# A last sum spread 16 partitions apart: one copy and a store of eight runs in place of four copies and a store of two rows

## The chip, the core and the metric

The kernel runs on one core of a Trainium2 chip. The metric is the device time of one execution in microseconds (us); the median over several runs counts, and a smaller one is better. The core's engines each work through their own queue in order: TensorE (PE; PEld for its weight loads), VectorE (DVE), ScalarE (ACT), GpSimd (POOL) and SyncE (SP), which here issues transfers. Data lies in DRAM, in SBUF (128 partitions) and in PSUM (128 partitions, where PE writes its sums).

## The reference

Two batch rows `x` of 448 numbers are normalised to `xn`. Then

- A: one decode step of attention with 16 query heads, 8 key and value heads of 256, over the last 4096 positions of the caches: `q = xn @ wq`, `softmax(q k / 16) v`, then `@ wo` (4096 x 448).
- B: a dense layer with the mish activation: `h = xn @ w1 + b1` (1792 wide), `h * tanh(softplus(h))`, then `@ w2` (1792 x 448).

The output is `x + A + B`, two rows of 448 in bf16. The K and V windows, the weights and little else are read: 77.67 MB.

## The kernel before, in words

All loads of K, V and the weights are issued by SP, in the order in which the code stands (the kernel runs under a manual schedule: each engine takes its instructions in program order). Three ring buffers of 32 KB a partition hold K, V, wq, w1 and w2 in turn.

The attention runs over four units `u` (0 to 3), each with two of the eight heads for both batch rows. For a unit, `turns` transposes K on VectorE (L275), `scores` multiplies (L362), takes the exponential on ScalarE and transposes the result, `weigh` sums the denominators, `values` multiplies with V (L408), `gather` brings the parts together, and `finish` (L450) divides and writes the bf16 tile `oT` on VectorE (L453). For the first three units `relay` and `mix_early` put the product with wo into the PSUM tile `early` (2 x 448), which also starts with `x`.

The end of the kernel uses a second PSUM tile, `acc` (L238). The 448 output columns are cut into G = 4 groups of 112, and group g stands in partitions 32g and 32g + 1, one for each batch row, so that the four groups' matmuls use four column groups of PE. `carry` (L240) copies `early` into `acc` through a 2 x 2 identity `id2`. `add_rows` (L253) adds a product: for each group a matmul whose fixed operand `lhsT` has 128 partitions and 2 columns and whose moving operand is 112 columns of a weight. It is called by `mix` (L495) for the last unit (8 calls, 32 matmuls) and by `dense_out` (L566) for w2 (14 calls, 56 matmuls). `dense_in` and `mish` have made `act_bf` (L502, L550) long before. w2 comes in four parts (L553, L561): 7, 4, 2 and 1 blocks of 448 columns, the last being the last load of all.

Behind the last matmul, `acc` is copied into the tile `res` (2 x 448, bf16) in four pieces of 2 x 112, two by VectorE (L626) and two by ScalarE (L628), and SP stores `res` (L629).

Of the kernel before, what the change touches and what calls it, by code (L numbers as in the profile page):

```python
# [9 lines left out]
ALU = mybir.AluOpType  # L10
AXIS = mybir.AxisListType
BF16 = mybir.dt.bfloat16
FP32 = mybir.dt.float32
# [4 lines left out]
def kernel(  # L18
# [13 lines left out]
    nc = tc.nc  # L32
    P = 128
    G = 4
# [4 lines left out]
    Bsz, Sq, D = A_x.shape  # L39
# [3 lines left out]
    rep = Hq // Hkv  # L43
# [3 lines left out]
    KU = J // Bsz  # L47
    U = Hkv // KU
# [12 lines left out]
    F2 = F // 2  # L61
    NI = F2 // P
    DG = D // G
    assert Sq == 1 and Bsz == 2 and rep == 2 and Dh == 256 and G * DG == D and Hq == 16
    assert W == 4096 and D == 448 and F == 1792
    scale = float(Dh) ** -0.5
# [9 lines left out]
    consts = ctx.enter_context(tc.tile_pool(name="consts", bufs=1))  # L76
    small = ctx.enter_context(tc.tile_pool(name="small", bufs=2))
# [32 lines left out]
    def load_wo(u):  # L110
# [22 lines left out]
        out=wq[:, 0 : NS * HW], in_=A_wq.flatten().rearrange("(p e) -> p e", p=P)  # L133
# [4 lines left out]
    ident = consts.tile([P, P], BF16)  # L138
# [6 lines left out]
    nc.vector.tensor_copy(  # L145
        out=halves[:], in_=ident[0:2, 0:2].unsqueeze(2).to_broadcast([2, 2, Bsz])
    )
    id2 = consts.tile([Bsz, Bsz], FP32)
    nc.vector.tensor_copy(out=id2[:], in_=ident[0:Bsz, 0:Bsz])
    hot = consts.tile([P, KU, 4, rep, 32, KU], BF16)  # L150
    nc.gpsimd.memset(hot[:], 0.0)
    for k in range(KU):
        nc.gpsimd.tensor_copy(
            out=hot[:, k, :, :, :, k],
            in_=ident[:].rearrange("p (q y) -> p y q", y=4).unsqueeze(2)
# [11 lines left out]
        out=rstd[:], in_=mv[:, 1:2], func=ACT.Sqrt, bias=eps_t[:], scale=1.0  # L167
# [4 lines left out]
        out=xn_bf[:],  # L172
        in0=x_bf[:],
# [7 lines left out]
        out=parm[:], in_=ident[:].rearrange("p (a o) -> p o a", o=2), axis=AXIS.X, op=ALU.add  # L181
# [3 lines left out]
        out=jm[:],  # L185
        in_=ident[:].rearrange("p (a j h) -> p j a h", j=J, h=rep),
        axis=AXIS.XY,
        op=ALU.add,
    )
    nc.vector.tensor_scalar(  # L190
        out=jm[:], in0=jm[:], scalar1=-1.0, scalar2=29952.0, op0=ALU.add, op1=ALU.mult
# [3 lines left out]
        out=mneg[:], in_=jm[:].unsqueeze(1).to_broadcast([P, TH * 8, J])  # L195
    )
    sel = consts.tile([P, 2, NQ], FP32)
    for x in range(2):
        for w in range(4):
            at = 32 * w + (2 * (w % 2) + x) * NQ  # L200
            src = ident[:, at : at + NQ]
            if w == 0:
                nc.vector.tensor_copy(out=sel[:, x, :], in_=src)
            else:
                nc.vector.tensor_tensor(
                    out=sel[:, x, :], in0=sel[:, x, :], in1=src, op=ALU.add
# [16 lines left out]
    for odd in range(2):  # L223
        for half in range(2):
            o = (half + odd) % 2
            nc.vector.tensor_scalar(
                out=xs[:, odd::2, half * Bsz : (half + 1) * Bsz],
                in0=xr_ps[:, odd::2, :],
# [8 lines left out]
    )  # L237
    acc = ps_a.tile([P, DG], FP32)  # L238

    def carry():  # L240
        e_sb = small.tile([P, 2 * Dh], FP32, tag="vs", name="e_sb", bufs=1)[0:Bsz, 0:D]
        nc.scalar.copy(out=e_sb, in_=early[:])
        for g in range(G):
            nc.tensor.matmul(
                acc[32 * g : 32 * g + Bsz, :],
                lhsT=id2[:],
                rhs=e_sb[:, g * DG : (g + 1) * DG],
                start=True,
                stop=False,
                skip_group_check=True,  # L250
            )

    def add_rows(lhsT, rows, stop=False):  # L253
        for g in range(G):
            nc.tensor.matmul(  # L255
                acc[32 * g : 32 * g + Bsz, :],
                lhsT=lhsT,
                rhs=rows[:, g * DG : (g + 1) * DG],
                start=False,
                stop=stop,  # L260
                skip_group_check=True,
            )
# [20 lines left out]
    for n in range(2):  # L283
        for e in range(2):
# [3 lines left out]
                out=sp[:],  # L288
                in_=ident[:, o : o + 63 : 2].unsqueeze(1).to_broadcast([P, G, 32]),
# [91 lines left out]
    state = {}  # L381
# [67 lines left out]

    def finish(u):  # L450
        po, rec = state.pop(("o", u)), state.pop(("rec", u))
        oT = small.tile([P, 2, KU * rep, Bsz], BF16, tag="oT", name="oT")
        nc.vector.tensor_tensor(  # L453
            out=oT[:].rearrange("p c k b -> p c b k"),
            in0=po[:].rearrange("p c (b k) -> p c b k", b=Bsz),
            in1=rec[:].rearrange("p (b k) -> p b k", b=Bsz).unsqueeze(1)
            .to_broadcast([P, 2, Bsz, KU * rep]),
            op=ALU.mult,
        )
        state["oT", u] = oT  # L460
# [34 lines left out]
    def mix(u):  # L495
        oT, w = state.pop(("oT", u)), wo_t.pop(u)
        for k2 in range(KU):
            for h in range(rep):
                for c in range(2):
                    add_rows(oT[:, c, k2 * rep + h, :], w[:, k2, h, c * D : (c + 1) * D])  # L500

    act_bf = consts.tile([P, NI, 2, Bsz], BF16)  # L502

    def load_w1():
        t = ring("w1")
# [29 lines left out]
    def mish():  # L535
        h_ps = state.pop("h")
        shape = [P, NI, 2, Bsz]
        u_sb = consts.tile(shape, FP32, name="u_sb")
        nc.scalar.activation(out=u_sb[:], in_=h_ps[:], func=ACT.Exp)
        t_sb = consts.tile(shape, FP32, name="t_sb")  # L540
        nc.vector.scalar_tensor_tensor(  # L541
            out=t_sb[:], in0=u_sb[:], scalar=2.0, in1=u_sb[:], op0=ALU.add, op1=ALU.mult
        )
        den = consts.tile(shape, FP32, name="den_sb")
        nc.vector.tensor_scalar(
            out=den[:], in0=t_sb[:], scalar1=2.0, scalar2=None, op0=ALU.add
        )
        nc.vector.reciprocal(out=den[:], in_=den[:])
        nc.vector.tensor_tensor(out=t_sb[:], in0=t_sb[:], in1=den[:], op=ALU.mult)
        nc.vector.tensor_tensor(out=act_bf[:], in0=h_ps[:], in1=t_sb[:], op=ALU.mult)  # L550

    KH = 4096
    w2_parts = ((0, 0, NI), (1, 0, 4), (1, 4, 6), (1, 6, NI))  # L553
# [12 lines left out]
    def dense_out(part):  # L566
        k, lo, hi = w2_parts[part]
        for i in range(lo, hi):
            at = k * KH + i * D
            add_rows(  # L570
                act_bf[:, i, k, :], state["w2"][:, at : at + D], stop=(k == 1 and i == NI - 1)
            )

    load_w1()
# [3 lines left out]
    turns(0, 1)  # L578
    dense_in()
    mish()  # L580
    scores(0, 1)
    weigh(0)
    for u in range(U - 1):
        load_k(u + 1, 0)
        load_v(u, 0)
        load_k(u + 1, 1)
        load_v(u, 1)
        load_wo(u)
        turns(u + 1, 0)
        values(u, 0)  # L590
        scores(u + 1, 0)
        turns(u + 1, 1)
        values(u, 1)
        gather(u)
        finish(u)
        scores(u + 1, 1)
        relay(u)
        mix_early(u)
        if u < U - 2:
            weigh(u + 1)  # L600
    u = U - 1
# [5 lines left out]
    for part in range(len(w2_parts)):  # L607
        load_w2(part)
    carry()
    values(u, 0)  # L610
    values(u, 1, 32)
    weigh(u)
    gather(u, last=False)
    values_fixed(u, 1, 32, 56)
    values_fixed(u, 1, 56, TV)
    finish(u)
    mix(u)
    for part in range(len(w2_parts)):
        dense_out(part)

    res = consts.tile([Bsz, D], BF16)
    for g in range(G):
        dst = res[:, g * DG : (g + 1) * DG]
        src = acc[32 * g : 32 * g + Bsz, :]
        if g % 2 == 0:
            nc.vector.tensor_copy(out=dst, in_=src)  # L626
        else:
            nc.scalar.copy(out=dst, in_=src)  # L628
    nc.sync.dma_start(out=out.flatten_outer_dims(), in_=res[:])  # L629


# [28 lines left out]
```

## Time and profile before

| | us |
|---|---|
| median of 4 runs | 189.36 |
| lowest and highest | 189.24, 189.54 |
| the profiled execution | 189.48 |
| its span | 187.5 |
| busy: VectorE, PE, ScalarE, GpSimd | 92.9, 74.3, 12.4, 4.7 |
| moved | 77.78 MB, 415 GB/s |

The span is the stretch from the first to the last instruction that the profiler recorded in one execution; the device time contains 1.98 us around it. A row of 40 digits shows busy tenths in 40 equal slices of the span, some 4.7 us each. A group's row gives line, engine, operation, output tile, input, count and nanoseconds; views of one line or tile give the shortest, median and longest of its instructions. A name with a small q (SPq) is the queue of an engine, which issues transfers or waits. Matmuls are pipelined, and their ends are modelled. The chain of waits is followed back from the last instruction: at each step to what released it.

### The profile page before, as it was taken

The page shows a single profiled execution, that of the slowest core. Times are in us where ns is not written, and L with a number is a line of the kernel's source. Part 1 is how long each engine was busy: PE and PEld are TensorE (multiplying, and loading weights), DVE is VectorE, ACT ScalarE, POOL GpSimd, SP SyncE. Part 2 cuts the span into 40 slices and gives each one's busy share as a digit, 9 for nine tenths or more (in the row PEclk, how much of TensorE's full clock was granted, in tenths as well). Part 3 has the DMA queues.
Part 4 walks back from the last instruction along what each step waited for, and adds up shares of the span by engine and source line. Part 5 has one row for each costly group of instructions (what it writes and reads, how often), then busy time and mean ns, then how long its engine had stood idle before and what let it go on. Part 6 is the DMA issues. An engine that isn't in the chain of part 4 may idle for free.

```text
span 187.5 us, 1952 instructions
## 1 busy us (share of the span) xinstructions
PE 74.3 (40%) x852; PEld 34.4 (18%) x856; DVE 92.9 (50%) x93; ACT 12.4 (7%) x26; POOL 4.7 (2%) x16
## 2 busy tenths in 40 slices
PE   0300367593119000882047002870068005854763
PEld 0100122451003000340012001430022002422452
DVE  6719624974792098028940395048910592040101
ACT  3000030101000100110001000110001000120101
POOL 8100000000000000000000000000000000000000
PEclk9999999999999955699559855798556655899555
DMA  6999999999999999999999999999999999999991
GB/s 225 447 420 398 469 399 426 469 444 447 413 420 413 430 449 389 471 447 447 440 406 409 420 447 415 452 444 447 447 427 406 413 433 427 440 423 398 432 404 43
DMA packets 4451, 77.78 MB, mean 415 GB/s; under 512 B 470, under 2 KB 1244, under 8 KB 2012
## 3 DMA queue, kind: packets, MB, share of 16 engines
q1 hardware_dynamic: 4436, 77.66, 96.8%
q8 instruction: 6, 0.10, 0.2%
q14 instruction: 1, 0.01, 0.0%
q10 hardware_dynamic: 8, 0.01, 0.0%
HBM read 77.67 MB, written 0.00 MB: 414 GB/s over the span
## 4 chain that ended last, share of the span: by engine, by line
DMA 79%; DVE 12%; PE 4%; issue 3%; SPq 1%; DVEq 0%
DMA k<-in_A_k_cache_dram 44%; DMA v<-in_A_v_cache_dram 23%; DMA w<-in_B_w_dram 12%; DVE kt L275 12%; PE pv L408 4%; PE acc L255 1%; SPq L98 0%; SPq L132 0%; SPq L561 0%; DVEq L655 0%; DVE res L626 0%; DVE t_sb L541 0%
## 5 line engine op out<-in xcount | busy, mean ns | idle before, releaser
L275 DVE STREAM_TRANSPOSE kt<-k 128x4096 f32<-128x4096 f32 x16 | 70.1, 4417 | 35.6 <-DMA k<-in_A_k_cache_dram 35.5
L408 PE MATMUL pv<-v,p 128*32 128x512 bf16 x240 | 24.1, 571 | 73.5 <-DMA v<-in_A_v_cache_dram 73.5
L408 PEld LDWEIGHTS <-p 128*32 128x32 bf16 x240 | 8.7, 129 | 86.6 <-issue 63.4
L362 PE MATMUL sc<-kt,qd 128*32 128x512 bf16 x256 | 20.1, 457 | 1.8 <-DVE qd L330 1.4
L453 DVE TENSOR_TENSOR oT<-o,rec 128x16 bf16<-128x16 f32 x4 | 0.7, 175 | 23.5 <-PE o L426 19.1
L373 DVE STREAM_TRANSPOSE p<-ex 128x512 bf16<-128x512 bf16 x8 | 5.2, 690 | 10.8 <-ACT ex L370 10.8
L370 ACT ACTIVATE ex<-sc 128x512 bf16<-128x512 f32 x8 | 4.8, 597 | 75.6 <-PE sc L362 75.6
L362 PEld LDWEIGHTS <-qd 128*32 128x32 bf16 x256 | 6.9, 107 | 12.3 <-issue 6.9
L297 PE MATMUL q_ps<-wq,xs 128*32 128x512 bf16 x28 | 3.2, 629 | 13.2 <-DMA wq<-in_A_wq_dram 13.2
L394 DVE TENSOR_REDUCE rec<-dn 128x8 f32<-128x512 f32 x4 | 2.8, 692 | 11.2 <-PE dn L386 9.8
L420 ACT COPY vs<-pv 128x512 f32<-128x512 f32 x4 | 2.3, 585 | 56.9 <-PE pv L408 56.9
L426 PE MATMUL o<-sel,vs 128*128 128x8 f32 x32 | 5.2, 289 | 2.1 <-ACT vs L420 2.1
L426 PEld LDWEIGHTS o<-sel,vs 128*128 128x128 f32 x32 | 4.8, 228 | 5.5 <-ACT vs L420 5.5
L487 PE MATMUL early<-wo,ox 128*2 128x448 bf16 x24 | 5.0, 352 | 1.9 <-ACT ox L478 1.9
L525 PE MATMUL h_ps<-xs,w 128*128 128x4 bf16 x49 | 3.7, 196 | 2.3 <-DMA w<-in_B_w_dram 2.3
L386 PE MATMUL dn<-p,ones 128*128 128x512 bf16 x5 | 2.4, 526 | 4.1 <-DVE p L344 3.8
L218 PE MATMUL xr_ps<-ident,xrows 2*128 2x2 bf16 x7 | 1.0, 181 | 7.1 <-DVE xrows L217 7.1
L297 PEld LDWEIGHTS <-xs 128*32 128x32 bf16 x28 | 1.1, 137 | 14.9 <-issue 14.9
L525 PEld LDWEIGHTS <-w 128*128 128x128 bf16 x49 | 3.2, 149 | 2.5 <-DMA w<-in_B_w_dram 2.4
L351 PE MATMUL sc<-mneg,ident 128*128 128x512 bf16 x7 | 3.1, 443 | 0.0
L441 PE MATMUL o<-p,v 128*128 128x8 bf16 x64 | 1.9, 168 | 1.8 <-DMA v<-in_A_v_cache_dram 1.8
L145 DVE COPY halves<-ident 2x4 bf16<-2x4 bf16 x1 | 1.9, 1912 | 1.3 <-POOL ident masks.py:199 1.3
(67 smaller groups left out, 44.3 us busy)
## 6 DMA issues: line engine op xcount, KB each, us to landing
k<-in_A_k_cache_dram SPq DMA_DIRECT2D x8, 4096.0 KB, 27.5
v<-in_A_v_cache_dram SPq DMA_DIRECT2D x7, 4096.0 KB, 21.2
wq<-in_A_wq_dram SPq DMA_DIRECT2D x1, 3584.0 KB, 20.2
wo<-in_A_wo_dram SPq DMA_DIRECT2D x3, 896.0 KB, 21.6
v<-in_A_v_cache_dram SPq DMA_DIRECT2D x1, 2048.0 KB, 17.6
w<-in_B_w_dram SPq DMA_DIRECT2D x1, 1568.0 KB, 13.0
v<-in_A_v_cache_dram SPq DMA_DIRECT2D x1, 1536.0 KB, 21.7
wo<-in_A_wo_dram SPq DMA_DIRECT2D x2, 448.0 KB
```

The source lines that it names most:

```text
L275: nc.vector.transpose(out=kt[i][:, :, r, :, :], in_=t[:, r * KE : (r + 1) * KE].bitcast(FP32).rearrange("p (a c j) -> p a c j", c=P // (R ...
L297: nc.tensor.matmul(q_ps[32 * u : 32 * (u + 1), :], lhsT=xs[:, s, :], rhs=wq_t[s][:, u * 512 : (u + 1) * 512], start=(s == 0), stop=(s == N ...
L351: nc.tensor.matmul(sc[:].rearrange("p t c m -> p (t c m)"), lhsT=ident[:], rhs=mneg[:].rearrange("p a j -> p (a j)"), start=True, stop=Fal ...
L362: nc.tensor.matmul(sc[32 * w : 32 * (w + 1)].rearrange("p t c m -> p t (c m)"), lhsT=qd[:, u, 2 * n + e, :, :].rearrange("p g q -> p (g q) ...
L370: nc.scalar.activation(out=ex[:, :, :, i, :], in_=sc[:], func=ACT.Exp, scale=scale)
L373: nc.vector.transpose(out=p_all[:, :, h * TH : (h + 1) * TH, :].rearrange("p g t q -> p t g q"), in_=ex[:, h * TH : (h + 1) * TH].rearrang ...
L386: nc.tensor.matmul(dn[:].rearrange("p a q -> p (a q)"), lhsT=ones[:], rhs=p_run[:, i].rearrange("p t q -> p (t q)"), start=(i == 0), stop= ...
L394: nc.vector.tensor_reduce(out=rec[:], in_=dn[:].rearrange("p a q -> p q a"), axis=AXIS.X, op=ALU.add)
L408: nc.tensor.matmul(pv[32 * w : 32 * (w + 1), :, :].rearrange("p x d -> p (x d)"), lhsT=p_run[:, g, 4 * a : 4 * a + 4, :].rearrange("p t q ...
L426: nc.tensor.matmul(po[:, c, :], lhsT=sb[:, x, c::2], rhs=sel[:, x, :], start=(x == 0 and c == 0), stop=(last and x == 1), skip_group_check ...
L487: nc.tensor.matmul(early[:], lhsT=ox[:, i, :], rhs=w[:, i, :], start=False, stop=(u == U - 2 and i == 7),)
L525: nc.tensor.matmul(h_ps[:, i, :, :].rearrange("p k b -> p (k b)"), lhsT=w1_v[:, s, i, :], rhs=xs[:, s, 0 : 2 * Bsz], start=False, stop=(s ...
```

## The change

The batch rows of a group now stand SP = 32 / 2 = 16 partitions apart, in partitions 32g and 32g + 16. To that end the fixed operands become tiles `[128, 2, 16]` in which the columns of batch row 0 stand in places 0 to 15 and those of row 1 in places 16 to 31, and column i is taken with the 17 columns from i to i + 16: its first is row 0's, its last row 1's, and what the 15 between add to other partitions of `acc` is not read. `id2` gets the same form with 32 columns. Unused places are set to zero by three memsets on VectorE at the start. Then partitions 0 to 112 of `acc` are copied at once, and every 16th partition of the copy is stored: eight runs of 112 numbers.

```diff
+    SP = 32 // Bsz
...
-    id2 = consts.tile([Bsz, Bsz], FP32)
-    nc.vector.tensor_copy(out=id2[:], in_=ident[0:Bsz, 0:Bsz])
+    id2 = consts.tile([Bsz, Bsz, SP], FP32)
+    nc.vector.memset(id2[:], 0.0)
+    nc.vector.tensor_copy(out=id2[:, :, 0], in_=ident[0:Bsz, 0:Bsz])
+    act_bf = consts.tile([P, Bsz, SP], BF16)
+    nc.vector.memset(act_bf[:], 0.0)
+    o_bf = consts.tile([P, Bsz, SP], BF16)
+    nc.vector.memset(o_bf[:], 0.0)
...
+    def spaced(t, i):
+        return t[:].rearrange("p b i -> p (b i)")[:, i : i + SP + 1]
...
-                acc[32 * g : 32 * g + Bsz, :],
-                lhsT=id2[:],
+                acc[32 * g : 32 * (g + 1), :],
+                lhsT=id2[:].rearrange("p b i -> p (b i)"),
...
-                acc[32 * g : 32 * g + Bsz, :],
+                acc[32 * g : 32 * g + SP + 1, :],
...
-        oT = small.tile([P, 2, KU * rep, Bsz], BF16, tag="oT", name="oT")
+        if u < U - 1:
+            oT = small.tile([P, 2, KU * rep, Bsz], BF16, tag="oT", name="oT")
+            oT_out = oT[:].rearrange("p c k b -> p c b k")
+        else:
+            oT = o_bf
+            oT_out = oT[:, :, 0 : 2 * KU * rep].rearrange("p b (c k) -> p c b k", c=2)
...
-                    add_rows(oT[:, c, k2 * rep + h, :], w[:, k2, h, c * D : (c + 1) * D])
-
-    act_bf = consts.tile([P, NI, 2, Bsz], BF16)
+                    i = (c * KU + k2) * rep + h
+                    add_rows(spaced(oT, i), w[:, k2, h, c * D : (c + 1) * D])
...
-        nc.vector.tensor_tensor(out=act_bf[:], in0=h_ps[:], in1=t_sb[:], op=ALU.mult)
+        nc.vector.tensor_tensor(
+            out=act_bf[:, :, 0 : 2 * NI].rearrange("p b (k i) -> p i k b", k=2),
+            in0=h_ps[:],
+            in1=t_sb[:],
+            op=ALU.mult,
+        )
...
-                act_bf[:, i, k, :], state["w2"][:, at : at + D], stop=(k == 1 and i == NI - 1)
+                spaced(act_bf, k * NI + i),
+                state["w2"][:, at : at + D],
+                stop=(k == 1 and i == NI - 1),
...
-    res = consts.tile([Bsz, D], BF16)
-    for g in range(G):
-        dst = res[:, g * DG : (g + 1) * DG]
-        src = acc[32 * g : 32 * g + Bsz, :]
-        if g % 2 == 0:
-            nc.vector.tensor_copy(out=dst, in_=src)
-        else:
-            nc.scalar.copy(out=dst, in_=src)
-    nc.sync.dma_start(out=out.flatten_outer_dims(), in_=res[:])
+    rows = 32 * (G - 1) + SP + 1
+    res = consts.tile([P, DG], BF16)
+    nc.vector.tensor_copy(out=res[0:rows, :], in_=acc[0:rows, :])
+    nc.sync.dma_start(
+        out=out.rearrange("b s (g d) -> g (s b) d", g=G), in_=res[0:rows:SP, :]
+    )
```

The number of matmuls, their moving operands, the loads and their order stay as they are.

More of the change, by code (lines that the diff above doesn't have):

```diff
@@ L451, in finish @@
         po, rec = state.pop(("o", u)), state.pop(("rec", u))
-        oT = small.tile([P, 2, KU * rep, Bsz], BF16, tag="oT", name="oT")
+        if u < U - 1:
[4 more added lines that the diff above has]
+            oT_out = oT[:, :, 0 : 2 * KU * rep].rearrange("p b (c k) -> p c b k", c=2)
         nc.vector.tensor_tensor(
-            out=oT[:].rearrange("p c k b -> p c b k"),
+            out=oT_out,
             in0=po[:].rearrange("p c (b k) -> p c b k", b=Bsz),
```

## The prediction

> **What bounds the kernel now.** I read the page first, for the whole span, then the chain of waits of the last 7.5 us, then the timeline of the last 3 us.
>
> ```profile
> DMA  6999999999999999999999999999999999999991
> ...
> DMA 79%; DVE 12%; PE 4%; issue 3%; SPq 1%; DVEq 0%
> ```
>
> The DMA row of the 40 slices is full from the second slice to the 39th: the transfer engines stream without a break from about 5 us to 183 us. So an edit that only lengthens or shortens an engine's work under that stream changes nothing; only what lies behind the last landing counts. The chain of waits shows that end (start, length, what):
>
> ```profile
> 160.93 22.76 DMA w<-in_B_w_dram
> 183.68 0.04 issue
> 183.72 0.54 PE acc L255 x16
> 184.27 0.03 issue
> 184.29 0.57 PE acc L255 x12
> ```
>
> The parts of w2 land at 183.68 and later, and PE starts 0.04 us behind each. The timeline from 184.5 us on shows that even these matmuls wait for landings:
>
> ```profile
> 184.29 0.53 PE L255 MATMUL acc<-w,act_bf 128*2 128x112 bf16 x12
> 184.56 0.09 PEld L255 LDWEIGHTS <-act_bf 128*2 128x2 bf16 x3
> 184.85 0.56 DVE L626 CAST res<-acc 2x112 bf16<-2x112 f32 x2 [3.27 <-PE acc L255]
> 184.89 0.51 ACT L628 CAST res<-acc 2x112 bf16<-2x112 f32 x2 [9.16 <-PE acc L255]
> 185.48 0.33 SPq L629 DMA_DIRECT2D out_dram<-res  x1
> ```
>
> The weight loads break off and start again at 184.56, where the last part (one group of four matmuls) has landed. From there the end is a plain row: four matmuls to 184.83, copies to 185.41, the store's issue from 185.48 to 185.81. In windows of 0.04 us the transfer engines then carry 22 GB/s in 186.20 to 186.28 and nothing later, and the span ends at 187.5, after the store's receipt and the shutdown. The profiled execution took 189.48 us, 1.98 us more than its span of 187.5; the median of the four runs is 189.36, 0.12 lower. I work out the difference against the profiled one and put it on the median.
>
> **The copies (removed from the end).** The view of the tile res:
>
> ```profile
> L626 DVE CAST res<-acc x2: 260/264/269, 184.9 to 185.1; 2x112 bf16<-2x112 f32 x2
> L628 ACT CAST res<-acc x2: 243/244/246, 184.9 to 185.2; 2x112 bf16<-2x112 f32 x2
> ```
>
> Two copies one behind the other on each engine take 0.56 us on VectorE and 0.51 on ScalarE, and the store waits for the later one. After the change one copy of 113x112 stands there. Does it cost more for 113 partitions? Copies out of PSUM give the answer: 128x16 takes 165 ns (L314), 2x112 takes 264, 32x256 takes 420 (L330). 96 more columns cost 99 ns and 144 more cost 156, 1.03 to 1.08 ns a column, whatever the partitions. So the new copy costs about 165 + 96 x 1.08 = 269 ns: it ends at 185.12 instead of 185.41. **Gain 0.56 - 0.27 = 0.29 us**, all of it on the path. ScalarE's copies end earlier and go too, with the store's wait for ScalarE; nothing else was behind them.
>
> The Trainium skill, page "TensorEngine Tiling (Array Packing)", section "PSUM Bottleneck", advises the opposite, to evacuate PSUM with ScalarE and VectorE both. If four copies' work stayed four copies' work on one engine, it would take 4 x 0.264 = 1.06 us, and this term would be a loss of 0.50 instead of a gain of 0.29; the rows above decide against that here.
>
> **The store (dearer).** Before, it is two rows of 896 bytes, plain on both sides. After, it is 8 runs of 224 bytes: SBUF partitions 16 apart, and on the DRAM side a nested pattern of 4 column groups x 2 rows. Its issue lies on the path. The length of an issue on SP, from the views of the lines:
>
> ```profile
> L629 SPq DMA_DIRECT2D out_dram<-res x1: 334/334/334, 185.5 to 185.5; - x1
> ...
> L98 SPq DMA_DIRECT2D k<-in_A_k_cache_dram x8: 534/535/632, 0.7 to 119.5; - x8
> ...
> L113 SPq DMA_DIRECT2D wo<-in_A_wo_dram x3: 597/597/598, 58.0 to 137.4; - x3
> ```
>
> Plain patterns (the store's two rows of 896 bytes, or w1's 128 rows of 12.5 KB, 337 ns at L506) cost 0.33 to 0.34; so neither rows nor bytes matter. Nested ones (k's 32 positions x 4 heads, wo's 64 x 2, the last wo's 128 x 2 with 462 to 586 ns at L119) cost 0.46 to 0.60. The new store is nested; I take 0.535, the median of k's 8 issues and of v's 10: **loss 0.20 us**. Ends: 0.243 (the plain bias load on ScalarE's queue, L128), a gain of 0.09; and 0.632 (the first k load), a loss of 0.30. That plain wq takes 0.575 near the start shows that the pattern is not all that decides, so a loss of nothing remains possible.
>
> Then the landing. The two old rows go by one transfer engine each, some 0.03 us apart: in the two windows 186.20 to 186.24 and 186.24 to 186.28 the share is 0.06 and 0.07, one engine of 16. Eight runs over up to eight engines put the last up to 6 x 0.03 = 0.18 us later; over four engines 2 x 0.03 = 0.06. I take **0.07 us** and keep 0 and 0.5 as ends. The 0.5 is SP's wait for the store in the view of waits, taken a second time in full, if small writes had to be answered one after the other.
>
> The skill's page "DMA: Bandwidth & Descriptors", section "Specifications", says that transfers under 512 bytes make the transfer engine read, modify and write; 896-byte rows become 224-byte runs here, so this rule speaks against the change. It gives no price, and no row here shows such a write; by it the landing would lean to its upper end and the sum to a loss.
>
> **The matmuls (17 columns instead of 2).** All 88 matmuls of L255 load 17 columns instead of 2, and four more with 32 columns stand in the carry. What the columns cost:
>
> ```profile
> L255 PEld LDWEIGHTS <-act_bf x56: 79/126/128, 182.2 to 184.6; 128*2 128x2 bf16 x56
> ...
> L408 PEld LDWEIGHTS <-p x240: 92/146/151, 47.7 to 174.1; 128*32 128x32 bf16 x120
> ```
>
> 32 columns instead of 2 cost 13 ns at the shortest and 20 at the median, so 15 more columns cost about 10. The moving side is the same 112 columns. Up to the last landing PE has pauses: it finishes 32 matmuls of L255 by 182.55 and the next 28 by 183.42, and waits for w2 until 182.60 and 183.72. A group of four takes about 0.09 us (28 matmuls, seven groups, in 0.82 us with the 0.25 of the last). Even four weight loads 10 ns longer each, with nothing of them hidden, add 0.04 a group, 0.16 us to the four groups at 183.72. Their last start is then about 184.13, before the landing at 184.29. So only the last group pays: **0.01 us** if its four column groups load side by side, with ends of 0 and 4 x 23 = 0.09 (151 less 128). Without the cover of the waits, 22 groups at 0.04 would be 0.88 us; this is the price if the landings were not the bound.
>
> **What is hidden.** At the start VectorE gets three memsets, and the copy of id2 then waits for one of them. A small memset there takes 59 ns (L159), while the neighbouring small copies take 1.9 us beside GpSimd's memsets. At worst this is 3 x 1.9 = 5.7 us in front of the layer norm and of the first K transposes. VectorE is idle for 4.35 us before those (13.21), so they could start 1.4 late; the w1 load behind them would be issued at 23.4 instead of 22.0, while the second k load keeps the queue fed until 31.33. PE needs xs at 21.8, and VectorE is done with it at 8.9. Cost 0. The strided output of act_bf (28 elements, 188 ns) is followed by 3.15 us of idle time before the next transposes: cost 0. The last oT goes to a fixed tile: the same operation of 175 ns, at 181.4 before a landing at 182.6, cost 0. The carry's four matmuls with 32 columns stand at 167.6, and the next work starts at 168.9: cost 0.
>
> **Sum.** -0.29 + 0.20 + 0.07 + 0.01 = -0.01 us: 189.47 for the profiled execution, **189.35** for the median. The copies' gain is paid back at the store.
>
> **Rivals.** A measurement of this kernel tells a difference of about 0.2% (0.38 us) from none.
> - *The store is not dearer*: the issue stays at 0.33, the landing at its place. Then the copies' gain stays: 189.36 - 0.29 = 189.07, still within 0.2%. For it speaks that L629 and L506 cost the same with 2 and 128 rows; against it, that no nested pattern in the trace is below 0.46.
> - *The store is the new bound and the kernel slower*: issue +0.26 (as wo) and small writes answered in turn, up to +0.5. With the matmuls' 0.01 that is 0.77 - 0.29 = +0.48: 189.84. It is slower by over 0.2% from a store that costs 0.67 more. For it: eight small runs instead of two; against it: two runs over different engines overlap in the windows.
> - *Faster by over 0.2%*: needs the store below its present cost, issue 0.243 and nothing else: 189.36 - 0.29 - 0.09 = 188.98. Only a plain load speaks for it.
> - *The copy does not do what is said*: if 113 partitions did cost per partition group, 1.06 us, the time would be 189.36 + 0.50 + 0.28 = 190.14; the 128x16 row speaks against it.
>
> **Numbers.** The wash (within 0.15 of 189.35) 0.56; the gain kept (189.0 to 189.2) 0.25; slower by over 0.2% through the store 0.09, through the copy 0.02; faster by over 0.2% 0.05; the last 0.03 lies between the wash and slower. So faster 0.05, same 0.84, slower 0.11. The range goes from the best store, 188.98, to 189.75, which leaves out most of the slower cases.
>
> **What would show it.** Right: one copy on VectorE of 0.25 to 0.29 us, with the store's issue starting near 185.19 if the last landing stays; that issue 0.46 to 0.60 long; the end of the span 2.2 to 2.4 us after the copy (2.05 before). Wrong: an issue of 0.33 (first rival), more than 0.3 us added between the store's packets and the end (second rival), a copy over 0.35 us, or the group of 16 at 183.72 reaching past the next landing. If the last landing itself moves by more than 0.3 us, the stream was changed by something that I have not seen here.

## The result and the profile after

| | before | after |
|---|---|---|
| median, us | 189.39 (55 runs) | 189.66 (37 runs) |
| lowest and highest | 189.18, 189.80 | 189.42, 189.91 |
| profiled execution | 189.48 | 189.77 |
| its span | 187.5 | 187.8 |

The ratio is 1.0014 with a 95% interval of 1.0009 to 1.0018: the changed kernel is slower by 0.27 us. The prediction had a change of -0.01. The loss is below the 0.2% that it called no change, and 189.66 lies inside its range (188.98 to 189.75), but the loss is clear of the measurement.

The stream is as full as before but for one of the 40 slices (8 tenths instead of 9): 77.78 MB at 414 GB/s, where it was 415.

```profile
DMA  6999999999999999999999999999999989999990
```

The end is still a plain row of steps. The timeline of the changed kernel from 184.5 us on (start, length, engine, line, operation; in brackets the idle time ahead and what ended it):

```profile
184.43 0.54 PE L264 MATMUL acc<-w,act_bf 128*17 128x112 bf16 x12
184.43 0.36 PEld L264 LDWEIGHTS <-act_bf 128*17 128x17 bf16 x11 [0.19 <-issue]
185.01 0.28 DVE L643 CAST res<-acc 113x112 bf16<-113x112 f32 x1 [3.30 <-PE acc L264]
185.31 0.68 SPq L644 DMA_DIRECT2D out_dram<-res  x1
```

One copy of 0.28 us stands where 0.56 stood, but the store's issue takes 0.68 us instead of 0.33. Where the store goes on from there is seen in the transfer engines' work, in windows (after the clock: share of the 16 engines, GB/s), of the changed kernel:

```profile
185.90:186.50 0.60, 0.00 (x0) 0.00 (x0) 0.00 (x0) 0.00 (x0) 0.00 (x0) 0.50 0.00 0
186.50:186.60 0.10, 0.00 (x0) 0.00 (x0) 0.00 (x0) 0.00 (x0) 0.00 (x0) 0.50 0.03 4
186.60:186.70 0.10, 0.00 (x0) 0.00 (x0) 0.00 (x0) 0.00 (x0) 0.00 (x0) 0.50 0.09 14
```

and of the kernel before:

```profile
185.80:186.20 0.40, 0.00 (x0) 0.00 (x0) 0.00 (x0) 0.00 (x0) 0.00 (x0) 0.50 0.00 0
186.20:186.30 0.10, 0.00 (x0) 0.00 (x0) 0.00 (x0) 0.00 (x0) 0.00 (x0) 0.50 0.05 18
```

The issue ends at 186.00, and the first packet moves at 186.59 by the trace's packet records. Before, the issue ended at 185.81 and the first packet moved at 186.24. So a second loss shows behind the issue. To compare executions whose last landing differs, I count from the start of the last group of four matmuls; I call the stretch from there to the end of the span the tail. Its steps, from the trace's records:

| step of the tail, us | before | after | difference |
|---|---|---|---|
| last group's start to the copy's start | 0.291 | 0.319 | +0.03 |
| copies | 0.561 | 0.275 | -0.29 |
| end of the copies to the store's issue | 0.063 | 0.027 | -0.04 |
| issue | 0.334 | 0.683 | +0.35 |
| end of the issue to the first packet | 0.426 | 0.594 | +0.17 |
| first packet to the last landing | 0.391 | 0.420 | +0.03 |
| last landing to the end | 0.836 | 0.835 | 0.00 |
| tail | 2.902 | 3.153 | **+0.25** |

The tail's 0.25 is nearly all of the loss of 0.27 us in the medians. In the two profiled executions the last group also starts 0.13 us later (184.69 against 184.56), but over the experiments below that start lies anywhere from 184.43 to 184.81, in kernels that load alike, so nothing is read from it.

### The profile page after: what moved, and what is told of

It is laid out like the page before. It is cut to its first block, busy times and chain, and to the rows that moved or that the text cites. A ratio compares the mean times of both kernels' runs of the same rounds, so it can differ in the third digit from the quotient of the medians.

```text
span 187.8 us, 1952 instructions
## 1 busy us (share of the span) xinstructions
PE 76.0 (40%) x852; PEld 34.9 (19%) x856; DVE 92.7 (49%) x95; ACT 12.0 (6%) x24; POOL 4.7 (2%) x16
## 2 busy tenths in 40 slices
DMA packets 4459, 77.78 MB, mean 414 GB/s; under 512 B 480, under 2 KB 1252, under 8 KB 2020
## 4 chain that ended last, share of the span: by engine, by line
DMA 57%; DVE 24%; PE 14%; ACT 2%; issue 1%; another core or an unknown queue 1%; SPq 0%
DMA v<-in_A_v_cache_dram 31%; DMA w<-in_B_w_dram 19%; DVE kt L284 19%; DMA k<-in_A_k_cache_dram 7%; PE pv L417 6%; PE sc L371 4%; DVE p L382 2%; PE h_ps L538 2%; PE o L435 1%; DVE rec L403 1%; ACT ex L379 1%; ACT vs L429 1%; PE acc L264 1%; DVE px L351 0%
## 5 line engine op out<-in xcount | busy, mean ns | idle before, releaser
L417 PE MATMUL pv<-v,p 128*32 128x512 bf16 x240 | 24.8, 585 | 72.2 <-DMA v<-in_A_v_cache_dram 72.2
L371 PE MATMUL sc<-kt,qd 128*32 128x512 bf16 x256 | 21.0, 474 | 1.8 <-DVE qd L339 1.4
L501 PEld LDWEIGHTS <-ox 128*2 128x2 bf16 x24 | 1.8, 83 | 4.1 <-ACT ox L492 2.2
```

What stands on the lines that cost most here:

```text
L371: nc.tensor.matmul(sc[32 * w : 32 * (w + 1)].rearrange("p t c m -> p t (c m)"), lhsT=qd[:, u, 2 * n + e, :, :].rearrange("p g q -> p (g q) ...
L417: nc.tensor.matmul(pv[32 * w : 32 * (w + 1), :, :].rearrange("p x d -> p (x d)"), lhsT=p_run[:, g, 4 * a : 4 * a + 4, :].rearrange("p t q ...
L501: nc.tensor.matmul(early[:], lhsT=ox[:, i, :], rhs=w[:, i, :], start=False, stop=(u == U - 2 and i == 7),)
```

## The experiments

The first theory was the prediction's own: a store that is nested on the DRAM side (4 groups x 2 rows) has a long issue (A). Its rivals: eight short runs cost as such, in whatever pattern (B), and the 17 columns shift the matmuls or the stream (C). Times are medians, with the ratio to runs of the kernel before on the same chip.

**The store without nesting.** The eight runs go to DRAM one behind the other, so the output is permuted.

```diff
-        out=out.rearrange("b s (g d) -> g (s b) d", g=G), in_=res[0:rows:SP, :]
+        out=out.rearrange("b s (g d) -> (b s g) d", g=G), in_=res[0:rows:SP, :]
```

> The changed kernel, but the store writes its eight runs one behind the other (row after row of partitions, a pattern of 8 x 112 on both sides), so the output is permuted. Theory A, the nested pattern costs: the issue falls from 0.68 to about 0.34 us and the stretch from its end to the first packet from 0.59 to about 0.43; the kernel then takes some 0.25 us less than before. Theory B, eight short runs cost as such, in whatever pattern: the issue stays near 0.68, and the kernel some 0.27 us over before. Theory C, the loss lies in the matmuls or the stream ahead of the store: the store is as long as before the change, and the loss stays all the same.

Measured: 189.65 us against 189.37, ratio 1.0016 (1.0007 to 1.0024). The view of the tile res (shortest, median, longest):

```profile
L643 DVE CAST res<-acc x1: 275/275/275, 185.0 to 185.0; 113x112 bf16<-113x112 f32 x1
L644 SPq DMA_DIRECT2D out_dram<-res x1: 725/725/725, 185.3 to 185.3; - x1
```

The issue is as long without the nesting, the first packet comes 0.591 us behind it, and the loss stays. A alone can't be the cause.

**Two stores.** One for each batch row: four runs from partitions 32 apart, plain on both sides.

```diff
-    nc.sync.dma_start(
-        out=out.rearrange("b s (g d) -> g (s b) d", g=G), in_=res[0:rows:SP, :]
-    )
+    for b in range(Bsz):
+        eng = nc.sync if b == 0 else nc.scalar
+        eng.dma_start(
+            out=out[b, 0, :].rearrange("(g d) -> g d", g=G),
+            in_=res[b * SP : b * SP + 32 * (G - 1) + 1 : 32, :],
+        )
```

> The changed kernel, with two stores, one for each batch row: 4 runs of 224 bytes each, plain on both sides, one issued by SP and one by ScalarE. Theory A: each issue takes 0.24 to 0.34 us, the two side by side; the copies' 0.29 us is kept, so 0.2 to 0.3 us less than before. Theory B: four short runs each cost half of what eight do over two, so about 0.5 us an issue and a time equal to before within 0.1. Theory C: 0.27 us over before, as the changed kernel.

Measured: 190.09 against 189.37, ratio 1.0036 (1.0022 to 1.0050), slower than either theory had it.

```profile
L646 SPq DMA_DIRECT2D out_dram<-res x1: 663/663/663, 185.3 to 185.3; - x1
L646 ACTq DMA_DIRECT2D out_dram<-res x1: 581/581/581, 185.3 to 185.3; - x1
```

Half the runs don't halve the issue. The two stores also hinder each other: ScalarE's first packet moves at 186.50, SP's only at 186.86, 0.92 behind the end of its issue, though SP began first. The stretch from the last landing to the end grew from 0.84 to 0.94. On its way out SP passes five waits one behind the other, here and in the kernel before. By the trace's records the landing before releases the last of the five; here the last landing releases the third, and two more waits of 0.06 each follow it.

**The 17 columns alone.** The end is as before, with copies from partitions 32g and 32g + 1, so that the second output row is another sum.

```diff
-    rows = 32 * (G - 1) + SP + 1
-    res = consts.tile([P, DG], BF16)
-    nc.vector.tensor_copy(out=res[0:rows, :], in_=acc[0:rows, :])
...
+    res = consts.tile([Bsz, D], BF16)
+    for g in range(G):
+        dst = res[:, g * DG : (g + 1) * DG]
+        src = acc[32 * g : 32 * g + Bsz, :]
...
+    nc.sync.dma_start(out=out.flatten_outer_dims(), in_=res[:])
```

> The changed kernel's 17 and 32 columns, memsets and tiles, with the end as before (four copies of 2 x 112 from partitions 32g and 32g + 1, and the store of two rows): the second output row is another sum than the wanted one. Theories A and B: equal to before within 0.06 us (about 0.03 in the last group). Theory C: some 0.27 us over before, the same as the whole change.

Measured: 189.41 against 189.37, ratio 1.0003 (0.9994 to 1.0012), no difference; the tail is 2.908 us against 2.902. The view of the matmuls' line:

```profile
L264 PEld LDWEIGHTS <-act_bf x56: 89/136/142, 182.2 to 184.6; 128*17 128x17 bf16 x56
L264 PE MATMUL acc<-w,act_bf x56: 250/297/301, 182.6 to 184.6; 128*17 128x112 bf16 x56
```

A weight load is 10 ns longer (89 and 136, where 2 columns had 79 and 126), the matmul as long as before. C falls.

**Four copies again.** The store as in the change, the copy cut into four of 17 x 112.

```diff
-    nc.vector.tensor_copy(out=res[0:rows, :], in_=acc[0:rows, :])
+    for g in range(G):
+        part = slice(32 * g, 32 * g + SP + 1)
+        if g % 2 == 0:
+            nc.vector.tensor_copy(out=res[part, :], in_=acc[part, :])
+        else:
+            nc.scalar.copy(out=res[part, :], in_=acc[part, :])
```

> The changed kernel with four copies of 17 x 112, two on VectorE and two on ScalarE, in place of the one of 113 x 112; the store as in the change. If one copy for four saves the time of the second copy, whatever its partitions, as the prediction had it: 0.28 us over the changed kernel, 0.55 over before. If copies of more partitions cost more, less than that.

Measured: 190.72 against 189.37, ratio 1.0068 (1.0055 to 1.0080). The loss is 1.35 us where 0.55 was expected, and the timeline shows most of the reason:

```profile
185.04 0.26 DVE L646 CAST res<-acc 17x112 bf16<-17x112 f32 x1 [3.32 <-PE acc L264]
185.33 0.24 ACT L648 CAST res<-acc 17x112 bf16<-17x112 f32 x1 [9.16 <-DVE res L646]
185.61 0.27 DVE L646 CAST res<-acc 17x112 bf16<-17x112 f32 x1 [0.31 <-ACT res L648]
185.91 0.24 ACT L648 CAST res<-acc 17x112 bf16<-17x112 f32 x1 [0.34 <-DVE res L646]
```

Each copy waits for the one ahead (the brackets name it), which the four copies into a tile of two partitions had not done. So this is no clean undoing of the one-copy part. It still gives two numbers: 17 x 112 takes 264 to 272 ns on VectorE, and 113 x 112 takes 275, so partitions cost next to nothing; and the copies' end is later by 0.845 us within the tail (1.439 against 0.594), of which the tail keeps all (3.999 against 3.153). Against the kernel before the tail is 1.10 longer; the other 0.25 of the 1.35 lies outside it and stays unexplained.

So the loss lies in the store and not in the matmuls, and taking the nesting away does not remove it; whether nesting has a price of its own is seen further down. What was left: the short run (E), the step between the partitions (F), the number of rows (G), and that the first store of a form is slow (D).

**Short runs from adjacent partitions.** The kernel before, storing 112 of the 448 columns of each row.

```diff
-    nc.sync.dma_start(out=out.flatten_outer_dims(), in_=res[:])
+    nc.sync.dma_start(out=out.flatten_outer_dims()[:, 0:DG], in_=res[:, 0:DG])
```

> The kernel before, storing only the first 112 columns of each row: two runs of 224 bytes from adjacent partitions; 336 columns of each output row are left out. The plain store of eight runs took 0.73 us to issue, and each of the two of four runs 0.66 and 0.58, so the nested pattern is not the cause; left are the short run (E), the step between partitions (F), the number of rows between 2 and 16 (G), and that the final store is the first of its form on its queue and so slow once (D). E: the issue is 0.6 to 0.7 us, the first packet 1.2 to 1.3 us after its start, and the kernel takes 0.5 us more than before. F and G: as before, 0.33 and 0.76, no difference. D: slow only if the form differs by run length.

Measured: 189.02 against 189.43, ratio 0.9978 (0.9969 to 0.9986).

```profile
184.85 0.56 DVE L626 CAST res<-acc 2x112 bf16<-2x112 f32 x2 [3.27 <-PE acc L255]
184.88 0.51 ACT L628 CAST res<-acc 2x112 bf16<-2x112 f32 x2 [9.20 <-PE acc L255]
185.14 0.32 SPq L629 DMA_DIRECT2D out_dram<-res  x1
```

The gain was not expected and has another cause: the store now waits for the first copy alone and starts at 185.14 instead of 185.48, beside the second copies. The issue is 0.32 and the first packet comes 0.75 us after its start, so a run of 224 bytes doesn't make it long, nor do rows that lie 896 bytes apart in DRAM. E falls.

**Eight runs from adjacent partitions.** The changed kernel, but partitions 0 to 7 are stored, seven of which hold other sums.

```diff
-        out=out.rearrange("b s (g d) -> g (s b) d", g=G), in_=res[0:rows:SP, :]
+        out=out.rearrange("b s (g d) -> (b s g) d", g=G), in_=res[0 : 2 * G, :]
```

> The changed kernel, its store taking partitions 0 to 7 of the copy instead of every 16th: eight runs of 224 bytes, plain, no step between partitions; seven of the eight runs of the output are other sums. F: the issue is back at 0.33 us and the kernel 0.25 under before. E and G: as the plain store of every 16th, issue near 0.7 and 0.28 over before.

Measured: 189.14 against 189.43, ratio 0.9989 (0.9980 to 0.9998); the tail is 2.640 us.

```profile
184.92 0.27 DVE L643 CAST res<-acc 113x112 bf16<-113x112 f32 x1 [3.33 <-PE acc L264]
185.22 0.36 SPq L644 DMA_DIRECT2D out_dram<-res  x1
```

Against the plain store of every 16th partition only the step is gone: the issue falls from 0.725 to 0.362 us, the stretch to the first packet from 0.591 to 0.426. G falls, F stands.

**The step alone.** The kernel before, with the store of two rows of 896 bytes taken from partitions 0 and 16 of a taller tile; the second row is zero.

```diff
+    res = consts.tile([32, D], BF16)
+    nc.gpsimd.memset(res[:], 0.0)
...
-    res = consts.tile([Bsz, D], BF16)
...
-        dst = res[:, g * DG : (g + 1) * DG]
+        dst = res[0:Bsz, g * DG : (g + 1) * DG]
...
-    nc.sync.dma_start(out=out.flatten_outer_dims(), in_=res[:])
+    nc.sync.dma_start(out=out.flatten_outer_dims(), in_=res[0:17:16, :])
```

> The kernel before, its store taking partitions 0 and 16 of a tile of 32 instead of 0 and 1: two runs of 896 bytes, one step of 16 partitions between them; the second output row is zero. F: issue 0.6 to 0.7 us, 0.5 us over before. E and G: issue 0.33, no difference.

Measured: 190.01 against 189.43, ratio 1.0033 (1.0020 to 1.0045). The issue is 0.746 us:

```profile
L630 SPq DMA_DIRECT2D out_dram<-res x1: 746/746/746, 185.7 to 185.7; - x1
```

Two runs, 896 bytes, plain, and a step: +0.41 in the issue, +0.17 to the first packet (0.592). The rest of the tail's 0.66 is the copies' end (+0.04) and one more wait ahead of the store (0.106 instead of 0.063).

**The store rehearsed.** The changed kernel with the same store once more, of zeros, 10 us ahead.

```diff
+    blank = consts.tile([P, DG], BF16)
+    nc.gpsimd.memset(blank[:], 0.0)
...
+    nc.sync.dma_start(
+        out=out.rearrange("b s (g d) -> g (s b) d", g=G), in_=blank[0 : 32 * (G - 1) + SP + 1 : SP, :]
+    )
     carry()
```

> The changed kernel with one store more: the same pattern of eight runs, from a tile of zeros, issued on SP's queue behind the last load of w2, some 10 us ahead of the final store, which overwrites it. D, the first store of a form is slow: the final store's issue falls to about 0.33 us, its first packet comes 0.76 us after the start, and the kernel takes 0.2 to 0.3 us less than before. E, F and G: the final store is as long as without it, and the kernel some 0.27 us over before.

Measured: 189.76 against 189.43, ratio 1.0019 (1.0010 to 1.0028). The view of the DRAM tensor shows the rehearsal and the final store:

```profile
L631 SPq DMA_DIRECT2D out_dram<-blank x1: 688/688/688, 174.9 to 174.9; - x1
L649 SPq DMA_DIRECT2D out_dram<-res x1: 580/580/580, 185.2 to 185.2; - x1
```

The rehearsed store is issued in 0.580 us, 0.10 less than in the change; D had 0.33. So the form is long the second time too, and about 0.1 of the 0.683 at most is D's. Whether that 0.1 falls on the first store of a form or on every one that does not follow its own form directly, the runs do not separate. The kernel before has two loads of the last wo directly one behind the other; by the trace's records the first of them took 0.586 and the second 0.462:

```profile
L119 SPq DMA_DIRECT2D wo<-in_A_wo_dram x2: 462/524/586, 156.6 to 157.2; - x2
```

But wo's three loads at L113, with others between them, took 597 to 598 ns each, the first no longer than the rest. The rehearsed store's first packet comes only 0.07 us sooner after the start (1.209 against 1.277), and the stretch from the last landing to the end is 0.10 longer, for the reason seen with the two stores: the landing releases the third of SP's five waits, not the last.

**A step of two.** As the step alone, with partitions 0 and 2.

```diff
-    nc.sync.dma_start(out=out.flatten_outer_dims(), in_=res[0:17:16, :])
+    nc.sync.dma_start(out=out.flatten_outer_dims(), in_=res[0:3:2, :])
```

> The kernel before, its store taking partitions 0 and 2 of the tile of 32 (with 16 between, the issue took 0.75 us and the kernel 0.6 more); the second output row is zero. If any step other than one sends the issue the long way: issue 0.65 to 0.75 us, 0.5 to 0.6 over before. If the step's length counts: 0.33 to 0.4 and no difference.

Measured: 190.11 against 189.42, ratio 1.0035 (1.0023 to 1.0048).

```profile
L630 SPq DMA_DIRECT2D out_dram<-res x1: 747/747/747, 185.7 to 185.7; - x1
```

The first packet comes 0.599 us behind the issue. Whether the step is 2 or 16 doesn't matter; that it isn't one does.

**Adjacent rows through the edges of the groups.** A layout that keeps the one copy and the right output without a step: the batch rows stand in the last two partitions of an even group and the first two of the odd one behind it, 30 to 33 and 94 to 97. Two stores of four adjacent partitions, nested 2 x 2 on the DRAM side, bring them out.

```diff
+    PAD = 32 - Bsz
...
+    def edge(t, i, g):
+        at = Bsz * i + (PAD if g % 2 else 0)
+        return t[:, at : at + 32]
...
-    rows = 32 * (G - 1) + SP + 1
+    rows = 32 * (G - 1) + Bsz
...
-    nc.sync.dma_start(
-        out=out.rearrange("b s (g d) -> g (s b) d", g=G), in_=res[0:rows:SP, :]
-    )
+    for h in range(2):
+        eng = nc.sync if h == 0 else nc.scalar
+        eng.dma_start(
+            out=out[:, 0, 2 * h * DG : 2 * (h + 1) * DG].rearrange("b (g d) -> g b d", g=2),
+            in_=res[64 * h + PAD : 64 * h + PAD + 2 * Bsz, :],
+        )
```

> A layout in which the rows lie in adjacent partitions and one copy is enough: the fixed operands have 32 columns, and the two batch rows stand in the last two partitions of an even group and the first two of an odd one (30 to 33 and 94 to 97). One copy of 98 x 112, and two stores of four adjacent partitions, nested 2 x 2 on the DRAM side, from SP and ScalarE. If the step is what costs, and not the nesting: each issue 0.33 to 0.45 us and the tail up to the first packet as before; the copies' 0.26 are kept, less what two stores side by side and a second semaphore cost (0.3 and 0.1 in the run with two stores of every 32nd partition): 0.0 to 0.2 over or under before. If nesting costs too: issues of 0.55 and more, and 0.3 over before.

Measured: 190.05 against 189.42, ratio 1.0034 (1.0021 to 1.0046).

```profile
L649 SPq DMA_DIRECT2D out_dram<-res x1: 775/775/775, 185.3 to 185.3; - x1
L649 ACTq DMA_DIRECT2D out_dram<-res x1: 702/702/702, 185.3 to 185.3; - x1
```

The issues are long although the partitions are adjacent. Either nesting costs too, or the place of the first partition does.

**The store on ScalarE's queue.**

```diff
-    nc.sync.dma_start(
+    nc.scalar.dma_start(
```

> The changed kernel with its store issued by ScalarE's queue. If the long issue belongs to the store's form: 0.6 to 0.7 us there too (0.58 in the run with two stores), and 0.2 to 0.3 over before. If SP is slower at it: 0.25 to 0.35 and 0.1 to 0.2 under before.

Measured: 189.62 against 189.42, ratio 1.0010 (1.0001 to 1.0019).

```profile
L644 ACTq DMA_DIRECT2D out_dram<-res x1: 597/597/597, 185.3 to 185.3; - x1
```

The issue is 0.09 us less than on SP, and the first packet comes 0.642 behind it, 0.05 more. So SP is not the reason; a plain final store on this queue was not run.

**Nested, adjacent partitions.** The change's DRAM pattern, taken from partitions 0 to 7; seven runs are other sums.

```diff
-        out=out.rearrange("b s (g d) -> g (s b) d", g=G), in_=res[0:rows:SP, :]
+        out=out.rearrange("b s (g d) -> g (s b) d", g=G), in_=res[0 : 2 * G, :]
```

> The changed kernel with its nested pattern on the DRAM side (4 groups x 2 rows), but the runs taken from the adjacent partitions 0 to 7; seven of the eight runs of the output are other sums. With a plain pattern these partitions gave an issue of 0.36 us and a kernel 0.2 to 0.3 under before. If nesting costs an issue by itself, as the issues of k and wo (0.53 to 0.60) and the two stores of 30 to 33 and 94 to 97 (0.78 and 0.70) suggest: 0.55 to 0.78 us, and 0.1 to 0.3 over before. If those two stores were long for another reason: 0.36, and 0.2 to 0.3 under.

Measured: 189.82 against 189.32, ratio 1.0024 (1.0013 to 1.0035); tail 3.256 us.

```profile
L644 SPq DMA_DIRECT2D out_dram<-res x1: 786/786/786, 185.4 to 185.4; - x1
```

**Plain, adjacent partitions from 30.**

```diff
-        out=out.rearrange("b s (g d) -> g (s b) d", g=G), in_=res[0:rows:SP, :]
+        out=out.rearrange("b s (g d) -> (b s g) d", g=G), in_=res[30 : 30 + 2 * G, :]
```

> The changed kernel with a plain store of eight adjacent partitions that begin at 30 instead of 0; the output is other sums. If the place of the first partition costs: issue 0.7 us or more, 0.3 over before. If not: 0.36 us, and 0.2 to 0.3 under before, as from partitions 0 to 7.

Measured: 189.11 against 189.32, ratio 0.9988 (0.9979 to 0.9996); tail 2.638 us.

```profile
L644 SPq DMA_DIRECT2D out_dram<-res x1: 367/367/367, 185.1 to 185.1; - x1
```

The plain run from partitions 0 to 7 differs from the first of these two in the nesting alone (0.362 against 0.786 us), and from the second in the place alone (0.362 against 0.367). So the place costs nothing, and nesting alone makes the issue long. So for the final store, the runs show:

| pattern of a final store on SP | issue, us | to the first packet | tail |
|---|---|---|---|
| plain, adjacent: 2 rows (before) | 0.334 | 0.426 | 2.902 |
| plain, adjacent: 8 rows from 0, from 30 | 0.362, 0.367 | 0.426, 0.417 | 2.640, 2.638 |
| plain, step of 16: 8 rows | 0.725 | 0.591 | 3.182 |
| plain, steps of 16 and 2: 2 rows (four copies) | 0.746, 0.747 | 0.592, 0.599 | 3.558, 3.580 |
| nested, adjacent: 8 rows | 0.786 | 0.593 | 3.256 |
| nested, step of 16: 8 rows (the change) | 0.683 | 0.594 | 3.153 |

A final store that is plain on both sides and takes adjacent partitions has the short form. One departure from that gives the long form, 0.32 to 0.42 us more in the issue than a plain store of as many rows and 0.17 more behind it, and a second one adds nothing. The number of transfer engines is not the reason: by the completion writes in the packet records the short form had 2 (before) or 8 (plain, adjacent), the long form 2 (step, two rows), 4 (nested) or 8 (plain, step).

No version here beats the kernel before with the right output: the two runs of 0.2 to 0.3 us less stored other sums, and the one of 0.4 us less stored only a quarter of the output. Eight adjacent partitions touch at most two of the groups of 32, so they hold at most four of the eight wanted runs, and no single store of this kind can bring them all. What the queue does in the long form, and why a load's nested issue (0.535) is shorter than a final store's, stays open; up to about 0.1 may belong to a store that does not follow its own form. Plain loads at the start of the kernel, wq on SP with 0.575 and x on ScalarE with 0.527, were long too, and no run here shows why.

## Why the prediction was wrong, step by step

- *What bounds the kernel*: right. The stream is as full, and e.g. the columns alone (88 matmuls with longer weight loads) change nothing; what the tail gains or loses arrives in the median, within 0.15 us in every run but the four copies.
- *The copies, gain 0.29*: right. 0.561 became 0.275 (269 ns were worked out), and the store starts another 0.04 sooner because it waits for one engine instead of two. The Trainium skill's page "TensorEngine Tiling (Array Packing)", section "PSUM Bottleneck", advises to use ScalarE and VectorE both, and in the line behind it to vectorize the access across several tiles of a bank. The prediction took the first as speaking against the change; the one copy over four groups is what the second asks for, and here it won, since one copy of 113 partitions takes 275 ns and one of 2 takes 264.
- *The store's issue, loss 0.20*: **this step failed.** The term measured 0.35, outside even the prediction's upper end of 0.30. It took the price from k's and v's loads (0.535), and a final store in the long form took 0.68 to 0.79; a store that does not follow its own form may account for up to about 0.1 of the 0.15 missed, and the rest stays open. The stated reason, nesting, was half of it: nesting is enough for the long form (0.786 with adjacent partitions), but so is the step of 16 partitions, so that taking the nesting away wins nothing. The bound from the loads' rows could not show the step, because all of them go to adjacent partitions.
- *From the issue to the first packet*: **this step failed too**, a term that the sum did not have. Without a reason given, the stretch was left at its 0.43 of before; it measured 0.59. This 0.17 is the largest term of the miss of 0.26.
- *The landing, 0.07*: too dear; from the first packet to the last landing it took 0.42 instead of 0.39, so eight runs cost 0.03. The rule of the skill's page "DMA: Bandwidth & Descriptors", section "Specifications", that transfers under 512 bytes make the engine read, modify and write, shows no price here; whether such writes took place no run shows: 224-byte runs needed 0.34 us (two runs) and 0.40 (eight) from packet to landing, 896-byte rows 0.39.
- *The matmuls, 0.01*: weight loads 10 ns longer, as worked out; the last group to the copy's start took 0.03 more. The hidden edits stayed hidden: the columns' run, which has all of them, can't be told from the kernel before (0.9994 to 1.0012).
- *The sum*: -0.29 + 0.20 + 0.07 + 0.01 became -0.29 - 0.04 + 0.35 + 0.17 + 0.03 + 0.03 = +0.25. The result lies between the forecast's wash and the slower rival, where the prediction had put a chance of 0.03. That the total is still near the forecast is luck in part: the sum missed 0.32 at the store and behind it, and the smaller terms gave 0.06 back. Of the signs that it listed for being right, two failed: the issue was to take 0.46 to 0.60, and the span was to end 2.2 to 2.4 us after the copy, where 2.56 was measured. The rival's mechanism, a store that costs more than the copies save, was the right one; the larger part of its price, small writes answered in turn, did not appear.

## What to carry to other kernels

The last store's issue and the way to its first packet lie bare on the path, so its pattern has a price: before a layout is chosen for the copies' sake, look whether the store stays plain on both sides and over adjacent partitions. Eight short runs are nearly free (issue 0.362 against 0.334 us); a step or a nested side costs over half a microsecond here. When a price is taken from rows that look alike, ask what those rows share with the new one (load or store, what stood ahead on the queue, which partitions), and follow the row on to the first packet, not only to the end of the issue.

## What the runs showed of the hardware that was not expected

- The long form shows twice, for a single store on SP, whichever departure causes it: in the issue (0.68 to 0.79 us instead of 0.32 to 0.37) and between its end and the first packet (0.59 to 0.60 instead of 0.42 to 0.44). The rehearsed store had 0.58 and 0.63.
- Eight runs nested as 4 x 2 go over four transfer engines and the plain eight over eight, as the completion writes in the packet records show (4 and 8). This agrees with the Trainium skill's page "DMA: Bandwidth & Descriptors", section "Why a DMA increments its semaphore by 16 and not by 1", by which the slowest dimensions of both sides set the number; from packet to landing the two took 0.42 and 0.40 us.
- Two stores issued side by side by SP and ScalarE are not two halves: the later first packet came 0.35 us behind the earlier (0.27 in the edges' run). What SP waits for on its way out counts by its place: a store whose landing releases the third of five waits ended 0.94 us behind its landing, one that releases the last 0.83 to 0.84.
- Each further engine that the store waits for goes with some 0.04 us more between the copies' end and the issue: 0.027 with one, 0.063 with two, 0.106 with three.
